# Long convolution and a gated network on one core: the projections of the last 24 tiles as pairs of products with 64 output columns each

## The chip, the cores and the metric

The kernel runs on one core of a Trainium2 chip. A core has five engines that run side by side, each through a list of instructions of its own and in its order: TensorE (matrix products, PE in the profile, with its weight loads listed as PEld), VectorE (DVE), ScalarE (ACT), GpSimd (POOL) and SyncE (SP, which here only issues DMAs). They wait for one another through semaphores. TensorE reads its two operands from SBUF and writes its product to PSUM, which has eight banks of 512 float32 columns on 128 partitions. The metric is the device time of one execution, in microseconds (us); the median over the runs counts.

## The reference

Two blocks are computed one after the other, all in float32. The first is a long convolution; the second is a network of two layers, and the change is in the second.

```python
# first block: x, v are (4, 12480, 128)
h_filt = (np.maximum(pos_emb @ w1, 0.0) @ w2) * np.exp(-0.01 * pos)[:, None]
u = x * v
y = irfft(rfft(u, n=2*S) * rfft(h_filt, n=2*S))[:, :S, :]   # along the sequence
z = (x * y).reshape(49920, 128)
# second block: w_in is (128, 2048), w_out is (2048, 128)
h = z @ w_in
out = (h * np.cos(h)) @ w_out
```

Each of the 49,920 rows of z is multiplied by `w_in` (up to 2048 numbers), goes through h cos h, and is multiplied by `w_out` (down to 128 numbers).

## The kernel before

The convolutions are done as Fourier transforms written as matrix products, one batch entry after the other; their results go to a buffer `zd` in HBM. The network takes these rows in 98 tiles (`NALL` = 98): a tile is up to 128 rows of `zd` with four tokens each, so 512 tokens (416 in tile 0, 352 in tile 97). Inside a tile the 2048 hidden numbers are handled in 16 chunks (`NFC`) of 128.

For one tile, `moe_load` brings the rows into `zb`; `moe_turn` turns them with four transposes on TensorE (features then lie on partitions, tokens along the free dimension) and ScalarE copies them to `at`. For each chunk c:

- `moe_up` (line 740): TensorE multiplies chunk c of `w_in` (the stationary operand, 128x128) by `at` (the moving operand, 128x512) into a bank `ph`. ScalarE scales it and adds a quarter turn (`a`, line 746), VectorE rounds it (`k`, line 749), GpSimd subtracts (`f`, line 752).
- `moe_act` (line 755): ScalarE takes the sine (`cs`, line 757), VectorE multiplies it with `ph` (`gt`, line 759). With this `ph` is free again.
- `moe_down` (line 762): TensorE multiplies chunk c of `w_out` by `gt` and adds to the tile's accumulator, a bank named `acc` or `cv`; chunk 0 starts the sum and chunk 15 ends it.

At the end of a tile `moe_evict` copies the accumulator to `ot`, `moe_back` turns it back with four transposes and `moe_store` sends it out.

The order is written out by hand in one loop over all (tile, chunk) steps (lines 949 to 974). Step i issues the up product of chunk i, then the down product of the chunk four steps earlier (`LAG` = 4), then the sine and the gate of chunk i-1. After chunk 3 come the transposes of the next tile, after chunk 8 those that turn the previous tile's result back. Between the steps the loop issues pieces of the convolutions as long as there are any; by the time of the last 24 tiles they are done, and TensorE has only up products, down products and transposes left. Four banks rotate under the name `ph` (they serve the up products and both kinds of transposes), and four buffers under `gt`. So an up product waits until VectorE has taken the gate of the bank's previous user, and a gate is written only when the down product that read the buffer's previous content is done.

A float32 product is compiled into two passes: weight load, pass, weight load, pass. In the profile one product is therefore two MATMUL and two LDWEIGHTS records; a transpose is one of each. `128*128` in a PE row means 128 rows of the array (contraction) by 128 columns (output partitions), and `128x512` the moving operand.

Of the kernel before, what the change touches and what calls it, by code (L numbers as in the profile page):

```python
# [16 lines left out]
P = 128  # L17
# [13 lines left out]
def kernel(  # L31
# [46 lines left out]
    nc = tc.nc  # L78
# [16 lines left out]
    CB = D // 2  # L95
# [3 lines left out]
    NFC = DFF // P  # L99
# [4 lines left out]
    NALL = 1 + math.ceil((NROWS - R) / P)  # L104
# [608 lines left out]
        yield from i1_units(bank)  # L713


    ats, accs = {}, {}

    def first_row(n):
        return min(R + (n - 1) * P, NROWS) if n else 0
# [1 line left out]
    def rows_of(n):  # L721
        return first_row(n + 1) - first_row(n)
# [17 lines left out]
    def moe_up(pool, n, c):  # L740
        m = G * rows_of(n)
        ph = ps_h.tile([P, BANK], F32, name="ph")
        nc.tensor.matmul(ph[:, 0:m], w_in_sb[:, c * P:(c + 1) * P], ats[n][:, 0:m],  # L743
                         start=True, stop=True)
        a = pool.tile([P, BANK], F32, name="a", bufs=3)
        nc.scalar.activation(a[:, 0:m], ph[:, 0:m], AF.Identity,  # L746
                             bias=quarter[:, 0:1], scale=INV_TWO_PI)
        k = pool.tile([P, BANK], F32, name="k")
        nc.vector.tensor_scalar(out=k[:, 0:m], in0=a[:, 0:m], scalar1=ROUND,  # L749
                                scalar2=ROUND, op0=ALU.add, op1=ALU.subtract)  # L750
        f = pool.tile([P, BANK], F32, name="f")
        nc.gpsimd.tensor_tensor(f[:, 0:m], a[:, 0:m], k[:, 0:m], op=ALU.subtract)  # L752
        return ph, f, m
# [8 lines left out]
    def moe_down(n, c, gt):  # L762
        if c == 0:

            accs[n] = bank() if made[0] == B * NG and n % 2 else \
                ps_acc.tile([P, BANK], F32, name="acc")
        m = G * rows_of(n)
        nc.tensor.matmul(accs[n][:, 0:m], w_out_sb[:, c, :], gt[:, 0:m],  # L768
                         start=(c == 0), stop=(c == NFC - 1))

    def moe_evict(pool, n):
        m = G * rows_of(n)
# [27 lines left out]
    with tc.manual_schedule():  # L800
        with tc.tile_pool(name="psum", bufs=8, space=PSUM) as psum, \
                ExitStack() as first:
            def bank():
                return psum.tile([P, BANK], F32, name="ps")
# [97 lines left out]
            w_in_sb = wpool.tile([D, DFF], F32, name="w_in_sb")  # L902
            w_out_sb = wpool.tile([P, NFC, D], F32, name="w_out_sb")
# [45 lines left out]
        for i in range(len(steps) + LAG):  # L949
            if i < len(steps):  # L950
                n, c = steps[i]
                if n == 0 and c == NFC // 2:
                    load(1)
                if c == NFC - 4 and n + 2 < NALL:
                    load(n + 2)
                hidden[i] = moe_up(mpool, n, c)
            if i >= LAG:
                pn, pc = steps[i - LAG]
                moe_down(pn, pc, gates.pop(i - LAG))
                if pc == NFC - 1:  # L960
                    ots[pn] = moe_evict(mpool, pn)
            if 0 <= i - 1 < len(steps):
                gates[i - 1] = moe_act(mpool, *hidden.pop(i - 1))
            if i < len(steps):

                if c == (LAG - 1 if n else NFC - 2) and n + 1 < NALL:
                    moe_turn(mpool, n + 1)
                if c == NFC // 2 and n - 1 in ots:
                    obs[n - 1] = moe_back(mpool, n - 1, ots.pop(n - 1))
                if c == NFC // 2 + 2 and n - 1 in obs:  # L970
                    moe_store(n - 1, obs.pop(n - 1))
            owed += 1.0
            while owed > 0.0:
                owed -= next(conv, owed)
# [30 lines left out]
```

## Time and profile before

| what | us |
|---|---|
| median of 3 runs (lowest, highest) | 3761.64 (3761.51, 3764.51) |
| span of the profiled execution, first to last instruction | 3758.9 |
| PE busy in it | 3690.6 (98%) |
| PE weight loads busy | 2110.4 (56%) |
| DVE, ACT, POOL busy | 2773.7, 2508.2, 2557.6 |
| mean of one up-product pass, 512 columns moving | 0.593 |
| mean of one POOL subtraction `f` | 1.267 |

For the profiled execution the span is the only time given; it lies 2.7 us under the median of the runs. Busy times are sums of the records of an engine. The records of TensorE overlap, since a pass starts while the one before it is still draining, so what a pass costs is read from the distance between two starts and not from the record's length.

### The profile page before, as it was taken

How to read it: one execution, taken by the hardware profiler on the slowest of the kernel's cores; microseconds unless marked ns; L12 is line 12 of the kernel's file. 1: busy time of each engine (PE TensorE's matmuls, PEld its weight loads, DVE VectorE, ACT ScalarE, POOL GpSimd, SP SyncE). 2: the span in 40 equal slices, each digit the busy share in tenths (PEclk: the TensorE clock that was granted, in tenths of full speed). 3: DMA queues.
4: the chain of work that ended last, by engine and by line, in shares of the span. 5: the costliest groups of instructions: out<-in, count | busy, mean ns of one | idle time of the engine just before them, and what ended most of it. 6: DMA issues, size and time to landing. Idle time of an engine off the chain costs nothing.

```text
span 3758.9 us, 47177 instructions
## 1 busy us (share of the span) xinstructions
PE 3690.6 (98%) x13546; PEld 2110.4 (56%) x13546; DVE 2773.7 (74%) x5586; ACT 2508.2 (67%) x4660; POOL 2557.6 (68%) x2318
## 2 busy tenths in 40 slices
PE   7898999999999999999999999999999999999999
PEld 6777555555566556555565556555566544444444
DVE  8887997687866787788766776788765666666666
ACT  5757776766665557766665567666664677777777
POOL 6666776588845665688745664788644677777776
PEclk9999999999999999999999999999999999999999
DMA  6263551022203650122104530122105200000000
GB/s 167 64 185 107 155 167 33 25 72 79 72 12 91 181 151 12 40 79 77 52 18 128 180 105 21 52 79 76 38 21 172 76 23 17 17 23 18 17 23 13
DMA packets 209499, 276.14 MB, mean 73 GB/s; under 512 B 17111, under 2 KB 146535, under 8 KB 209111
## 3 DMA queue, kind: packets, MB, share of 16 engines
q1 hardware_dynamic: 209239, 273.12, 24.8%
q8 instruction: 109, 1.79, 0.2%
q14 instruction: 151, 1.24, 0.1%
HBM read 193.64 MB, written 79.42 MB: 73 GB/s over the span
## 4 chain that ended last, share of the span: by engine, by line
PE 88%; DVE 3%; POOL 3%; ACT 2%; DMA 2%; issue 1%; SPq 0%; POOLq 0%; DVEq 0%; ACTq 0%
PE ph L743 33%; PE acc L768 28%; PE cv L504 5%; PE cv L768 5%; PE cv L479 4%; PE cv L407 3%; PE cv L448 3%; PE ph L126 2%; POOL f L752 1%; PE ps L407 1%; PE ps L448 1%; DMA tm<-td 1%; DMA wd<-w 1%; ACT cs L757 1%; DVE k L749 1%
## 5 line engine op out<-in xcount | busy, mean ns | idle before, releaser
L752 POOL TENSOR_TENSOR f<-a,k 128x512 f32<-128x512 f32 (+1 forms) x1568 | 1986.2, 1267 | 1060.5 <-DVE k L749 1059.1
L743 PE MATMUL ph<-at,w_in_sb 128*128 128x512 f32 (+1 forms) x3136 | 1599.0, 591 | 3.7 <-DVE gt L759 2.7
L746 ACT ACTIVATE a<-ph,quarter 128x512 f32<-128x512 f32 (+1 forms) x1568 | 1071.2, 683 | 704.8 <-PE ph L743 695.2
L768 PE MATMUL acc<-gt,w_out_sb 128*128 128x512 f32 (+1 forms) x2688 | 1370.3, 591 | 0.0
L759 DVE TENSOR_TENSOR gt<-ph,cs 128x512 f32<-128x512 f32 (+1 forms) x1568 | 1077.3, 687 | 359.9 <-ACT cs L757 341.8
L757 ACT ACTIVATE cs<-f 128x512 f32<-128x512 f32 (+1 forms) x1568 | 981.0, 626 | 366.6 <-POOL f L752 364.3
L749 DVE TENSOR_SCALAR k<-a 128x512 f32<-128x512 f32 (+1 forms) x1568 | 792.9, 506 | 550.7 <-ACT a L746 524.2
L768 PEld LDWEIGHTS acc<-gt,w_out_sb 128*128 128x128 f32 x2688 | 508.4, 189 | 642.8 <-issue 631.9
L743 PEld LDWEIGHTS ph<-at,w_in_sb 128*128 128x128 f32 x3136 | 553.2, 190 | 337.7 <-issue 257.5
L474 POOL TENSOR_TENSOR slots<-slots,t 120x256 f32<-120x256 f32 x384 | 312.9, 821 | 59.9 <-DVE t L467 25.6
L504 PEld LDWEIGHTS cv<-slots,tm 96*104 96x104 f32 x1920 | 238.6, 169 | 106.8 <-issue 85.4
L504 PE MATMUL cv<-slots,tm 96*104 96x128 f32 x1920 | 251.7, 273 | 9.9 <-POOL tm L297 5.0
L768 PE MATMUL cv<-gt,w_out_sb 128*128 128x512 f32 (+1 forms) x448 | 224.5, 583 | 1.0 <-DVE gt L759 1.0
L479 PEld LDWEIGHTS cv<-cs,slots 120*96 120x96 f32 x1536 | 176.7, 167 | 67.2 <-issue 65.2
L479 PE MATMUL cv<-cs,slots 120*96 120x120 f32 x1536 | 183.2, 266 | 0.0
L448 PEld LDWEIGHTS cv<-slots,w 124*120 124x120 f32 x576 | 103.7, 184 | 124.3 <-issue 112.3
L407 PEld LDWEIGHTS cv<-c,slots 104*124 104x124 f32 x768 | 132.6, 192 | 72.2 <-issue 60.0
L448 PE MATMUL cv<-slots,w 124*120 124x256 f32 x576 | 173.0, 380 | 0.0
L407 PE MATMUL cv<-c,slots 104*124 104x192 f32 x768 | 151.8, 327 | 5.4 <-DVE gt L759 3.5
L768 PEld LDWEIGHTS cv<-gt,w_out_sb 128*128 128x128 f32 x448 | 84.9, 190 | 104.8 <-issue 99.5
L489 DVE TENSOR_TENSOR slots<-cv,other 96x240 f32<-96x240 f32 x384 | 133.1, 394 | 1.5 <-ACT other L487 1.4
L395 DVE TENSOR_TENSOR xt<-xt,vt 104x256 f32<-104x256 f32 x177 | 132.6, 751 | 0.6 <-DMA vt<-in_v_dram 0.6
(131 smaller groups left out, 2520.9 us busy)
## 6 DMA issues: line engine op xcount, KB each, us to landing
h<-hd SPq DMA_DIRECT2D x144, 240.0 KB
tm<-td SPq DMA_DIRECT2D x96, 312.0 KB
xt<-in_x_dram SPq DMA_DIRECT2D x120, 208.0 KB
vt<-in_v_dram SPq DMA_DIRECT2D x120, 208.0 KB
xs<-in_x_dram SPq DMA_DIRECT2D x120, 208.0 KB
zd<-zs SPq DMA_DIRECT2D x119, 208.0 KB
zb<-zd SPq DMA_DIRECT2D x96, 256.0 KB
w<-wd SPq DMA_DIRECT2D x144, 116.2 KB
```

The lines of the kernel that those rows point to most:

```text
L407: nc.tensor.matmul(ps[0:KE, i * 2 * N1:(i + 1) * 2 * N1], u[:, b, 0:KE, i], c1[0:u.shape[0], :, :].rearrange("p r k -> p (r k)"), start=Tr ...
L448: nc.tensor.matmul(pi, w[:, i, :], parts[0:KE, :, k], start=True, stop=True)
L474: nc.gpsimd.tensor_tensor(y[:, r], y[:, r], t[:, r], op=op)
L479: nc.tensor.matmul(ps[0:N1, (i * 2 + r) * N2:(i * 2 + r + 1) * N2], parts[0:N2, r, :, b, i], cs[:, r, :], start=True, stop=True)
L504: nc.tensor.matmul(ps[0:R, i * D:(i + 1) * D], t[:, i, r, :], slots[0:N1, :, place, :], start=(r == 0), stop=(r == 1))
L743: nc.tensor.matmul(ph[:, 0:m], w_in_sb[:, c * P:(c + 1) * P], ats[n][:, 0:m], start=True, stop=True)
L746: nc.scalar.activation(a[:, 0:m], ph[:, 0:m], AF.Identity, bias=quarter[:, 0:1], scale=INV_TWO_PI)
L749: nc.vector.tensor_scalar(out=k[:, 0:m], in0=a[:, 0:m], scalar1=ROUND, scalar2=ROUND, op0=ALU.add, op1=ALU.subtract)
L752: nc.gpsimd.tensor_tensor(f[:, 0:m], a[:, 0:m], k[:, 0:m], op=ALU.subtract)
L757: nc.scalar.activation(cs[:, 0:m], f[:, 0:m], AF.Sin, scale=TWO_PI)
L759: nc.vector.tensor_tensor(gt[:, 0:m], ph[:, 0:m], cs[:, 0:m], op=ALU.mult)
L768: nc.tensor.matmul(accs[n][:, 0:m], w_out_sb[:, c, :], gt[:, 0:m], start=(c == 0), stop=(c == NFC - 1))
```

## The change

Three places in the tile count are marked: `PAIRS` = 74, `HALVES` = 82, `TURNED` = 90. Up to tile 73 nothing is changed. From there on some products are split into two halves of 64 output columns: half 0 takes the left 64 columns of the weights and writes PSUM partitions 0 to 63, half 1 takes the right 64 and writes partitions 64 to 127. Both halves stream the same moving operand in full.

- Tiles 74 to 81: up products stay whole. The down product of an even chunk is put off until that of the next, odd chunk; then four halves are issued: (c-1, half 0), (c-1, half 1), (c, half 0), (c, half 1).
- Tiles 82 to 89: up and down products are both split, each chunk at its own step as before.
- Tiles 90 to 97: up products are split as in 82 to 89; down products are put off by pairs of chunks as in 74 to 81, in the order (c-1, half 0), (c, half 1), (c, half 0), (c-1, half 1).

The four transposes of a group stay whole (128 columns) everywhere. In the built program the halves are placed in a TensorE array divided into two parts of 128 rows by 64 columns, at column 0 and at column 64. Each half is again weight load, pass, weight load, pass. The other engines' instructions and their order are the same as before, and so is the number of semaphore waits on each engine.

```diff
+    PAIRS, HALVES, TURNED = NALL - 24, NALL - 16, NALL - 8
 ...
     def moe_up(pool, n, c):
-        nc.tensor.matmul(ph[:, 0:m], w_in_sb[:, c * P:(c + 1) * P], ats[n][:, 0:m],
-                         start=True, stop=True)
+        if n < HALVES:
+            nc.tensor.matmul(ph[:, 0:m], w_in_sb[:, c * P:(c + 1) * P], ats[n][:, 0:m],
+                             start=True, stop=True)
+        else:
+            for h in range(2):
+                nc.tensor.matmul(ph[h * CB:(h + 1) * CB, 0:m],
+                                 w_in_sb[:, c * P + h * CB:c * P + (h + 1) * CB],
+                                 ats[n][:, 0:m], start=True, stop=True)
 ...
     def moe_down(n, c, gt):
-        nc.tensor.matmul(accs[n][:, 0:m], w_out_sb[:, c, :], gt[:, 0:m],
-                         start=(c == 0), stop=(c == NFC - 1))
+        def part(cc, h, gt, start=False, stop=False):
+            nc.tensor.matmul(accs[n][h * CB:(h + 1) * CB, 0:m],
+                             w_out_sb[:, cc, h * CB:(h + 1) * CB], gt[:, 0:m],
+                             start=start, stop=stop)
+
+        if n < PAIRS:
+            nc.tensor.matmul(accs[n][:, 0:m], w_out_sb[:, c, :], gt[:, 0:m],
+                             start=(c == 0), stop=(c == NFC - 1))
+        elif HALVES <= n < TURNED:
+            for h in range(2):
+                part(c, h, gt, c == 0, c == NFC - 1)
+        elif c % 2 == 0:
+            pending[n] = gt
+        else:
+            last = pending.pop(n)
+            four = ((c - 1, 0, last), (c - 1, 1, last), (c, 0, gt), (c, 1, gt)) \
+                if n < TURNED else \
+                ((c - 1, 0, last), (c, 1, gt), (c, 0, gt), (c - 1, 1, last))
+            for i, (cc, h, g) in enumerate(four):
+                part(cc, h, g, c == 1 and i < 2, c == NFC - 1 and i >= 2)
```

More of the change, by code (lines that the diff above doesn't have):

```diff
@@ L713, in forward_units @@
         yield from i1_units(bank)
-    ats, accs = {}, {}
+    ats, accs, pending = {}, {}, {}
+    PAIRS, HALVES, TURNED = NALL - 24, NALL - 16, NALL - 8
     def first_row(n):
```

## The prediction

> **What bounds the kernel now.** I read the page's busy table and slices first, then three windows of eight tiles each (the 24 that change), then TensorE's timeline in them, and last the places where a weight load was not made ahead.
>
> ```profile
> PE 3690.6 (98%) x13546; PEld 2110.4 (56%) x13546; DVE 2773.7 (74%) x5586; ACT 2508.2 (67%) x4660; POOL 2557.6 (68%) x2318
> ...
> PEclk9999999999999999999999999999999999999999
> ```
>
> ```profile
> 3076.80:3303.60 226.80, 226.80 (x578) 103.53 (x577) 146.19 (x256) 176.84 (x281) 162.84 (x129) 1.00 0.07 19
> 3303.60:3530.30 226.70, 226.70 (x577) 103.48 (x576) 145.99 (x256) 176.79 (x281) 162.65 (x129) 1.00 0.07 19
> 3530.30:3758.90 228.60, 222.88 (x585) 104.43 (x583) 144.59 (x259) 173.09 (x284) 159.28 (x130) 1.00 0.06 17
> ```
>
> In the windows (stretch; length, then busy us of PE, weight loads, DVE, ACT, POOL; granted clock, DMA share, GB/s) PE is never idle while the tiles stream, at the full clock. ACT, next, is busy 78% (176.84 of 226.80). A tile costs 226.8/8 = 28.35 us. Whatever TensorE needs more here is added to the end; what the others do is covered up to 22%.
>
> ```profile
> 3600.34 1.02 PE L768 MATMUL acc<-gt,w_out_sb 128*128 128x512 f32 x2
> 3601.20 1.02 PE L743 MATMUL ph<-at,w_in_sb 128*128 128x512 f32 x2
> 3602.05 1.02 PE L768 MATMUL acc<-gt,w_out_sb 128*128 128x512 f32 x2
> 3602.91 0.60 PE L126 MATMUL ph<-ident,ot 128*128 128x128 f32 x4
> 3603.35 1.02 PE L743 MATMUL ph<-at,w_in_sb 128*128 128x512 f32 x2
> ```
>
> Starts are 0.859 us apart per product (two passes of 0.429) and 0.43 per four transposes; 32 x 0.859 + 2 x 0.43 = 28.35. A pass's record is 0.592 long, so 0.163 of it drains under the next pass. Between transposes and products nothing is lost.
>
> ```profile
> 3629.97 0.19 PEld L768 LDWEIGHTS cv<-gt,w_out_sb 128*128 128x128 f32 x1 [0.24 <-issue]
> 3630.40 0.19 PEld L768 LDWEIGHTS cv<-gt,w_out_sb 128*128 128x128 f32 x1 [0.24 <-issue]
> ```
>
> Each load starts with a pass and is done 0.19 later, ahead of its own pass. Where a load could not be made ahead it shows in the product:
>
> ```profile
> 3741.11 0.86 PE L743 MATMUL ph<-at,w_in_sb 128*128 128x352 f32 x2
> 3741.81 0.76 PE L768 MATMUL cv<-gt,w_out_sb 128*128 128x352 f32 x2
> ```
>
> The first waited for a gate with its load: 0.86 against 0.76, so an exposed load of 128 columns costs 0.10. Last, what a pass's length depends on:
>
> ```profile
> L448 PE MATMUL ps<-slots,w 124*120 124x256 f32 x192 | 62.2, 405 | 7.0 <-DVE w L293 6.5
> ...
> L451 PE MATMUL ps<-ftile,w 124*120 124x256 f32 x96 | 29.4, 387 | 0.0
> L357 PE MATMUL ps<-w_sb,slots 128*96 128x256 f32 x120 | 26.1, 379 | 0.8 <-ACT slots L350 0.8
> ```
>
> With 256 elements moving, 96 output columns take 379 ns and 120 take 387 to 405: the moving elements set it, the columns do not. So a half of 64 columns should last as long as a whole product, and all hangs on whether two halves stream beside each other.
>
> **The change, part by part.**
>
> 1. Passes. Split are 8 x 16 = 128 down products in tiles 74 to 81 and 8 x 32 in each of the next two groups: 640 products become 1280 halves, 2560 passes of 0.429 in place of 1280. If the two halves of the array work at once, passes h0-1, h0-2, h1-1, h1-2 (half, pass) come in this order: h0-2 needs h0-1 done, h1-1 can start with h0-2, h1-2 runs beside the next product's h0-1. Two passes always run together and a product still costs 0.859: 0 us. If they run one after the other, 608 x 0.859 + 32 x 0.592 (the 352-column tile, two passes of 0.296) = 541 us. No matmul of before is narrow enough to stand beside another, so the ends are 0 and 541. I take 0: the halves have disjoint columns, disjoint PSUM partitions, no semaphore between them, and the nearest thing in the trace, weight load beside pass, overlaps perfectly.
>
> 2. Half-empty ends. In that pattern the first pass of a run of halves and the last stand alone: n products take 2n + 1 slots. Counting the built order, there are 93 runs between whole products or transposes: 61 of four halves (tiles 74 to 81), 32 longer ones cut by transposes, two groups per tile. 93 x 0.429 = 40 us.
>
> 3. Switching between whole and halved array, 186 times. From below: 0, as between transposes and products. From above: a drained pass and an exposed load, 0.163 + 0.10 = 0.27, so 50 us. I take the 0.163, since a whole product and a half overlap in columns as no two neighbours of before differ: 30 us. The Trainium skill (TensorEngine Tiling (Array Packing), Key Properties) says that changing the tiling mode drains the engine, which no row here can show; it speaks against this change, and by its drain alone the sum would be the same, without it 30 us less.
>
> 4. Weight loads. 1280 loads become 2560 of 64 columns. Two per slot of 0.429 fit even at the 0.19 measured for 128 columns. I take 0. The upper bound is that a load is never made past a pass still waiting: then h1's loads start only when h0-2 has, and each half pays one exposed load, 1280 x 0.05 to 0.10 (half of the 0.10, by columns, or all) = 64 to 128 us.
>
> 5. Waits on gates and banks. By pairs, two ups now stand back to back, then 1.72 us of downs. An up's gate is done 5.02 us after the up starts (timeline: up at 3672.06, a 3673.12, k 3673.91, f 3674.42, cs 3675.72, gt 3676.38 + 0.69 = 3677.07). The tightest taker of a bank comes three ups later with transposes between: before 3 x 1.717 + 0.43 = 5.58. After: two ups 1.72, four halves 1.72 + 0.43 + 0.33 (steps 2 and 3), transposes 0.43, one up 0.86: 5.48, against 5.02 + 0.10 for its load. No stall. Were steps 2 and 3 free it would be 4.72, short by 0.40, three times a tile in 16 tiles: 19 us, the bound; behind the waiting up stand TensorE's downs. GpSimd, 1.27 per chunk, delays the second chunk of a pair by 1.27 - 0.86 = 0.41; its bank is wanted a block of downs later (6.4). The put-off down holds its `gt` until up + 1.72 + 0.43 + 0.16; VectorE wants to overwrite it 4.32 after the previous up's start, 0.3 later: 0. Behind that gate on DVE would stand the next chunk's rounding, and GpSimd behind that.
>
> 6. Tail. The last four halves all follow the last gate: 5 slots of 0.296 in place of 2, 0.9 us. DMAs, stores and the queues of SP and POOL keep their order: 0.
>
> Sum: 0 + 40 + 30 + 0 + 0 + 1 = +71, span 3758.9 to 3830. The median lies 2.7 above the span: 3833 us, 1.9% slower. Own range, with steps 2 to 5 at their ends: 3762 + 40 to 3762 + 110, 3802 to 3872.
>
> The Trainium skill (TensorE: Matmul & The Clock Gate, Measured speedup vs the span model) gives 2.38x for three column tiles of 512 elements, 0.79 of the ideal. An estimate with that efficiency on all 640 products, 640 x 0.859 x (1/0.79 - 1), would be +146 us. No run here shows it, and step 1 is not taken from it.
>
> **The rivals.**
>
> - Loads in strict order (step 4's bound): +71 + 64 to 128, 3897 to 3961. For it: in this trace no load ever starts before the pass ahead of it has. Against it: there was never a second place to load into, so that row can't tell.
> - Half overlap: h1-1 runs beside h0-2, but h1-2 doesn't stand beside the next product's first pass. Three slots per product: 608 x 0.429 + 32 x 0.296 = 270, plus the 30 of switching: 4062. For it: ups wait on semaphores at their first load. Against: whole products with the same waits follow each other without a gap.
> - No overlap: +541, plus 0 to 30: 4303 to 4333. Gates would then all be early and TensorE still the bound. For it: every two passes in the trace are a full 0.429 apart. Against: all of them need the same columns.
> - Not slower: passes of 64 columns are shorter than 0.429. It decides from the point where 640 x 0.859 = 550 us shrinks by 71, a pass of 0.374. Against it the equal times at 96 and 120 columns; I know of nothing for it. At a pass of 0.35 the time would be 3833 - 550 x 0.185 = 3731.
>
> **How the numbers follow.** Overlap with costs at the ends 0.48, strict loads 0.22, half overlap 0.10, no overlap 0.15, not slower 0.05. The time is the first one's, 3833. The range leaves out no overlap and not slower, 0.20, and runs from the first one's lower end less a few us for a clock or start that differs to half overlap's: 3795 to 4065. A measurement of this kernel tells about 0.2% (7.5 us) from no change; every case but the last is slower by more, and the last I split: faster 0.03, same 0.02, slower 0.95.
>
> **What would show it.** The same three windows, by tiles: if I am right the first eight take 226.8 + 61 x 0.755 = 273 us, the next two 8-tile groups 16 x 0.755 = 12 more each (0.755 = 0.429 + 2 x 0.163), with starts of half 1's first pass and half 0's second within some 0.01. Strict loads: those starts 0.05 to 0.10 apart, 0.05 to 0.10 per half on top, 13 to 26 in the first group and 26 to 51 in each of the others. Half overlap: 1.29 per split product; no overlap: 1.72, and the second group 447 us or more. Step 3 shows in the first start after each run, step 5 as idle PE before an up, released by `gt`. I am wrong if half passes are not 0.429, if which `gt` the two halves read matters (then the third group differs from the second), or if the granted clock falls with both halves busy.

## The result, and the profile after

The changed kernel takes 3799.45 us (median; 3796.12 to 3800.12) against 3763.07 for the kernel before (3761.51 to 3765.24): 1.0097 times as long, 95% interval 1.0083 to 1.0111, so 31 to 42 us more. The forecast was slower, 3833 us in a range of 3795 to 4065. The direction and the mechanism (halves run beside each other) hold; the predicted rise of 71 us is about twice the 36 measured.

The page of the profile after, engine totals and TensorE's granted clock:

```profile
PE 3725.2 (98%) x14826; PEld 2036.1 (54%) x14826; DVE 2808.1 (74%) x5586; ACT 2493.7 (66%) x4660; POOL 2561.5 (68%) x2318
...
PEclk9999999999999999999999999999999999999999
```

1280 more passes than before (14826 against 13546), and yet only 34.6 us more of PE busy time; the clock is unchanged. The next view is TensorE's timeline of the changed kernel, cut to the transposes that turn the next tile: the first number is the start in us, and the distance of two such lines is one tile. The pairs stand in tiles 74 to 81, 82 to 89 and 90 to 97.

```profile
3111.73 0.66 PE L126 MATMUL ph<-ident,zb 128*128 128x128 f32 x4
3143.43 0.66 PE L126 MATMUL ph<-ident,zb 128*128 128x128 f32 x4
...
3361.84 0.65 PE L126 MATMUL ph<-ident,zb 128*128 128x128 f32 x4
3390.78 0.65 PE L126 MATMUL ph<-ident,zb 128*128 128x128 f32 x4
...
3593.80 0.66 PE L126 MATMUL ph<-ident,zb 128*128 128x128 f32 x4
3623.19 0.66 PE L126 MATMUL ph<-ident,zb 128*128 128x128 f32 x4
```

31.70, 28.94 and 29.39 us a tile, where before it is 28.34:

```profile
3112.03 0.60 PE L126 MATMUL ph<-ident,zb 128*128 128x128 f32 x4
3140.37 0.60 PE L126 MATMUL ph<-ident,zb 128*128 128x128 f32 x4
```

Most of the loss is in the first group, where whole and halved products alternate; in the second group all products are halved and a tile loses 0.60.

Where a tile of the first group loses it, in the same timeline, with the weight loads (PEld) below:

```profile
3175.13 0.66 PE L126 MATMUL ph<-ident,zb 128*128 128x128 f32 x4
3175.62 1.02 PE L745 MATMUL ph<-at,w_in_sb 128*128 128x512 f32 x2
3176.89 1.12 PE L745 MATMUL ph<-at,w_in_sb 128*128 128x512 f32 x2 [0.24 <-ACT at L738]
...
3177.94 1.94 PE L777 MATMUL cv<-gt,w_out_sb 128*64 128x512 f32 x8
3179.81 1.98 PE L745 MATMUL ph<-at,w_in_sb 128*128 128x512 f32 x4
```

```profile
3177.94 0.20 PEld L777 LDWEIGHTS cv<-gt,w_out_sb 128*64 128x64 f32 x4 [0.76 <-issue]
3178.42 0.14 PEld L777 LDWEIGHTS cv<-gt,w_out_sb 128*64 128x64 f32 x2 [0.29 <-issue]
3178.85 0.14 PEld L777 LDWEIGHTS cv<-gt,w_out_sb 128*64 128x64 f32 x2 [0.28 <-issue]
3179.81 0.30 PEld L745 LDWEIGHTS ph<-at,w_in_sb 128*128 128x128 f32 x2 [0.81 <-DVE k L756]
```

Three things are to be seen. First, eight half-passes (`x8`) take 1.94 us from first start to last end, where four whole passes take 1.88 in a row (four starts 0.429 apart and 0.592 for the last): two halves cost one whole product. Four loads start within 0.06 us at 3177.94, then two per 0.43. The passes themselves start 0.006 to 0.007 us apart in pairs (3177.942 and 3177.949, 3178.422 and 3178.429, 3178.852 and 3178.858, 3179.281 and 3179.287). Eight passes fill four slots, not the five that the prediction counted: there is no half-empty slot at either end. Second, around the run of halves time goes to the switch: from the last whole pass at 3177.42 to the first half it is 0.52 in place of 0.429, the first half slot is 0.48, the last one to the next load 0.53, and the first whole pass after it 0.53 because its load is exposed. The four excesses are 0.093, 0.051, 0.098 and 0.104: about 0.345 us per run. Around a group of transposes inside halved tiles (the lines below) they are 0.098, 0.055, 0.093 and 0.051: 0.297. Third, the second up product behind the transposes starts at 3176.89 and not at 3176.48; it waits for ScalarE's copy `at`, and its exposed load makes it 1.12 long.

```profile
3447.70 1.03 PE L777 MATMUL cv<-gt,w_out_sb 128*64 128x512 f32 x4
3448.66 0.66 PE L126 MATMUL ph<-ident,zb 128*128 128x128 f32 x4
3449.24 1.08 PE L749 MATMUL ph<-at,w_in_sb 128*64 128x512 f32 x4
```

At the end of the kernel three of the last four halves (six passes) follow the last gate (`gt`). First the changed kernel, then the one before:

```profile
3787.80 1.40 PE L777 MATMUL cv<-gt,w_out_sb 128*64 128x352 f32 x6 [0.40 <-DVE gt L766]
3789.74 0.64 PE L126 MATMUL ph<-ident,ot 128*88 128x128 f32 x4 [0.54 <-ACT ot L800]
```

```profile
3752.86 0.86 PE L768 MATMUL cv<-gt,w_out_sb 128*128 128x352 f32 x2 [0.35 <-DVE gt L759]
3754.27 0.64 PE L126 MATMUL ph<-ident,ot 128*88 128x128 f32 x4 [0.54 <-ACT ot L774]
```

From the first pass behind that gate to the last transposes it takes 1.94 us in place of 1.41, 0.5 more.

| in the changed kernel | count | us each | us |
|---|---|---|---|
| switches around a run of four halves (tiles 74 to 81) | 61 | 0.345 | 21.0 |
| switches around transposes (from tile 82 on) | 32 | 0.297 | 9.5 |
| waits of up products behind transposes, per tile, tiles 74 to 81 | 8 | 0.60 | 4.8 |
| the same, tiles 90 to 96 (behind tile 97 no tile is left to turn) | 7 | 0.45 | 3.2 |
| the end, behind the last gate | 1 | 0.5 | 0.5 |
| sum | | | 39.0 |

(0.60 is 31.70 - 28.34 - 8 x 0.345; 0.45 is 29.39 - 28.94.) From the transposes in tile 73 to the end the two profiled executions differ by 39.1 us; up to there, where nothing is changed, the one after was 3.7 us shorter.

### The profile page after: what moved, and what is told of

Its sections match the earlier page's. It is cut to its first block, busy times and chain, and to the rows that moved or that the text cites. A ratio compares the mean times of both kernels' runs of the same rounds, so it can differ in the third digit from the quotient of the medians.

```text
span 3794.3 us, 49737 instructions
## 1 busy us (share of the span) xinstructions
PE 3725.2 (98%) x14826; PEld 2036.1 (54%) x14826; DVE 2808.1 (74%) x5586; ACT 2493.7 (66%) x4660; POOL 2561.5 (68%) x2318
## 4 chain that ended last, share of the span: by engine, by line
PE 88%; DMA 3%; DVE 3%; POOL 2%; ACT 2%; issue 1%; SPq 0%; POOLq 0%; DVEq 0%; ACTq 0%
PE ph L745 29%; PE acc L782 24%; PE ph L749 5%; PE cv L504 5%; PE acc L777 4%; PE cv L479 4%; PE cv L777 4%; PE cv L448 3%; PE cv L407 3%; PE ph L126 2%; DMA hd<-h 2%; POOL f L759 1%; PE ps L407 1%; PE ps L479 1%; PE cv L782 1%
## 5 line engine op out<-in xcount | busy, mean ns | idle before, releaser
L745 PE MATMUL ph<-at,w_in_sb 128*128 128x512 f32 (+1 forms) x2624 | 1341.2, 595 | 5.5 <-ACT at L738 2.7
L756 DVE TENSOR_SCALAR k<-a 128x512 f32<-128x512 f32 (+1 forms) x1568 | 836.5, 533 | 559.9 <-ACT a L753 529.9
L782 PE MATMUL acc<-gt,w_out_sb 128*128 128x512 f32 (+1 forms) x2304 | 1174.1, 591 | 0.0
L782 PEld LDWEIGHTS acc<-gt,w_out_sb 128*128 128x128 f32 x2304 | 435.4, 189 | 552.2 <-issue 542.1
L745 PEld LDWEIGHTS ph<-at,w_in_sb 128*128 128x128 f32 x2624 | 453.2, 189 | 255.5 <-issue 137.3
L749 PE MATMUL ph<-at,w_in_sb 128*64 128x512 f32 (+1 forms) x1024 | 252.5, 588 | 1.7 <-DVE gt L766 0.6
L777 PE MATMUL acc<-gt,w_out_sb 128*64 128x512 f32 x768 | 188.1, 596 | 0.0
L777 PE MATMUL cv<-gt,w_out_sb 128*64 128x512 f32 (+1 forms) x768 | 185.0, 585 | 0.6 <-DVE gt L766 0.6
L749 PEld LDWEIGHTS ph<-at,w_in_sb 128*64 128x64 f32 x1024 | 70.1, 137 | 134.9 <-issue 101.8
```

Of the source, the lines that this page charges most:

```text
L749: nc.tensor.matmul(ph[h * CB:(h + 1) * CB, 0:m], w_in_sb[:, c * P + h * CB:c * P + (h + 1) * CB], ats[n][:, 0:m], start=True, stop=True)
L777: nc.tensor.matmul(accs[n][h * CB:(h + 1) * CB, 0:m], w_out_sb[:, cc, h * CB:(h + 1) * CB], gt[:, 0:m], start=start, stop=stop)
```

## The experiments

Three questions were open: is the rest really switches and nothing that halves cost by themselves; what is the wait behind the transposes; and why are the ends of a run not half empty, that is, in what order does TensorE take the passes. The theory was that each part of the divided array goes through its own instructions; the rivals are in the expectations. Where nothing else is said the edit is against the changed kernel, and a tile's time is the distance between its transposes as above.

### The transposes' bank

```diff
 def moe_turn(pool, n):
-        pt = ps_h.tile([P, BANK], F32, name="ph")
+        pt = bank() if n > PAIRS else ps_h.tile([P, BANK], F32, name="ph")
```

> Theory (switches and one bank): of the 39 us that the profile of the changed kernel has over before, about 8 are a wait of the second up product behind a tile's transposes, which takes over the transposes' bank and waits until ScalarE has copied it. Taking that bank from the three that are free by then removes the wait: tiles 74 to 81 go from 31.69 us to 31.1 to 31.2 (8 runs of halves at 0.345 on 28.34), tiles 90 to 97 from 29.39 to 28.94, tiles 82 to 89 stay at 28.94; the median falls by 7 to 8 us, to about 3792. Rival (the wait is for gates that come late because down products stand in pairs, or for the longer block of halves): the bank makes no difference, 3799 and the same tile times.

Measured: 3792.83 us, 1.0082 times before (1.0067 to 1.0097), 6.6 under the changed kernel. Its timeline, one tile of the first and one of the third group:

```profile
3111.76 0.66 PE L126 MATMUL cv<-ident,zb 128*128 128x128 f32 x4
3142.94 0.66 PE L126 MATMUL cv<-ident,zb 128*128 128x128 f32 x4
...
3618.98 0.66 PE L126 MATMUL cv<-ident,zb 128*128 128x128 f32 x4
3648.04 0.65 PE L126 MATMUL cv<-ident,zb 128*128 128x128 f32 x4
```

The first pair reads 31.18, the second 29.06; the second group of tiles stays at 28.94. So the theory holds: 0.5 us a tile in the first group and 0.33 in the third were the wait for that bank. What is left, 0.08 and 0.12, stands at the up product right behind the other transposes (those of `ot`), which waits for a gate; this is read from the timeline, no run takes it away in halves.

### By pairs, but whole

```diff
-    PAIRS, HALVES, TURNED = NALL - 24, NALL - 16, NALL - 8
+    PAIRS, HALVES, TURNED = NALL - 24, NALL, NALL
 ...
-        if n < HALVES:
+        if True:
 ...
-            for i, (cc, h, g) in enumerate(four):
-                part(cc, h, g, c == 1 and i < 2, c == NFC - 1 and i >= 2)
+            for cc, g in ((c - 1, last), (c, gt)):
+                nc.tensor.matmul(accs[n][:, 0:m], w_out_sb[:, cc, :], g[:, 0:m],
+                                 start=(cc == 0), stop=(cc == NFC - 1))
```

> Whole products everywhere, only the order by pairs is kept, in all of the last 24 tiles. Theory: no switch is left, and only the wait for the transposes' bank remains, 0.5 to 0.6 us a tile: tiles at 28.9, 3763 + 12 to 15 = 3775 to 3778. Rival 1 (the halves' blocks make the wait): tiles at 28.34 and 3763. Rival 2 (step 5 of the prediction, gates late three times a tile by 0.40): tiles at 29.5, 3792.

Measured: 3787.75 us, 1.0069 (1.0054 to 1.0084), 29.44 us a tile in all three groups: 1.10 a tile, neither the 0.6 of the theory nor the 1.2 of rival 2. The timeline shows two waits, not one:

```profile
3351.86 0.60 PE L126 MATMUL ph<-ident,zb 128*128 128x128 f32 x4
3352.30 1.02 PE L745 MATMUL ph<-at,w_in_sb 128*128 128x512 f32 x2
3353.71 1.12 PE L745 MATMUL ph<-at,w_in_sb 128*128 128x512 f32 x2 [0.38 <-ACT at L738]
3354.67 1.88 PE L795 MATMUL cv<-gt,w_out_sb 128*128 128x512 f32 x4
...
3360.68 0.60 PE L126 MATMUL ph<-ident,ot 128*128 128x128 f32 x4
3361.46 1.13 PE L745 MATMUL ph<-at,w_in_sb 128*128 128x512 f32 x2 [0.18 <-DVE gt L766]
```

The second up behind the first transposes starts 1.41 us after the one ahead of it in place of 0.86, and its load is exposed (1.12 against 1.02): 0.65. The first up behind the other transposes starts 0.78 after them in place of 0.43, with its load exposed: 0.45. The sum is the 1.10. In the changed kernel only 0.60 of the 1.10 is left. That its switches cover the rest, because they give the late copies and gates time, is argued and was not tested by itself. So by pairs costs more without halves (25 us over 24 tiles) than the waits cost with them.

Whether that is all was tried with the same kernel and both kinds of transposes in free banks (the same line is changed in `moe_turn` and in `moe_back`; the edit is against the run just above):

```diff
-        pt = ps_h.tile([P, BANK], F32, name="ph")
+        pt = bank() if n > PAIRS else ps_h.tile([P, BANK], F32, name="ph")
```

> The run with whole products and down products by pairs, but both kinds of transposes take a bank of the three that are free by then, so that the four banks of the up products rotate among up products alone. Theory (by pairs costs nothing but the two waits for banks behind the transposes, 0.65 and 0.45 us a tile, which are gone): tiles at 28.34 in place of 29.44, the median back at 3762 to 3764, no change from before. Rival (two up products in a row bring the gates late wherever they stand): part of the 1.10 us a tile stays, with waits for gates at other up products; tiles between 28.6 and 29.4, 3769 to 3788.

Measured: 3762.62 us, 1.0000 (0.9990 to 1.0009).

```profile
3368.94 0.60 PE L126 MATMUL cv<-ident,zb 128*128 128x128 f32 x4
3397.28 0.60 PE L126 MATMUL cv<-ident,zb 128*128 128x128 f32 x4
```

28.34 a tile, as before, from the third of the 24 tiles on. The first two take 28.81 and 28.82: there the transposes of `ot` still take one of the up products' banks (the `n > PAIRS` of the edit), and the 0.47 is their wait again. The order by pairs is free once the up products' banks are not lent to transposes; all its cost was banks.

### All halves, and how the cost goes with runs

In all 24 tiles up and down are split at each chunk (`PAIRS, HALVES, TURNED = NALL - 24, NALL - 24, NALL`):

> Up and down products split at each chunk in all of the last 24 tiles. Theory (each half of the array goes through its own instructions, so a run of halves has no half-empty end, and costs only its two switches, 0.297 us between transposes): 28.94 us in all 24 tiles, 24 x 0.60 = 14 us, 3777. Rival (half-empty ends of 0.429 per run, as predicted, hidden in the changed kernel by something): 24 x 2 x (0.297 + 0.429) = 35 us, 3798. Rival (two halves cost more than one whole product by a few ns each): the excess would be 768 products times that, on top of 14.

Measured: 3775.93 us, 1.0036 (1.0022 to 1.0050). The windows view of one tile (stretch; length, busy us of PE, loads, DVE, ACT, POOL; clock, DMA share, GB/s):

```profile
3371.02:3399.96 28.94, 28.94 (x138) 9.85 (x136) 18.03 (x33) 22.31 (x36) 20.48 (x17) 1.00 0.06 19
```

28.94 a tile (28.89 the first), two switched runs at 0.297 a tile and no more: 32 products a tile in halves cost nothing by themselves. Then the same with the up products whole (and `if True:` in `moe_up`), so that each tile has 16 runs of two halves:

> Up products whole, down products split at each chunk, in the last 24 tiles: 16 runs a tile of two halves in place of 8 runs of four. Theory (a run costs its two switches, 0.345 us, however long it is): tiles at 28.34 + 16 x 0.345 = 33.86, 3763 + 132 = 3895. Rival (the cost goes with the number of halves, 0.345/4 for each): 28.34 + 32 x 0.086 = 31.1, 3829. Rival (half-empty ends): 28.34 + 16 x (0.429 + 0.163 to 0.33) = 37.8 to 40.5, 3990 to 4055.

Measured: 3894.07 us in one run, 33.83 us a tile.

```profile
3439.57 1.12 PE L745 MATMUL ph<-at,w_in_sb 128*128 128x512 f32 x2
3440.62 1.08 PE L777 MATMUL acc<-gt,w_out_sb 128*64 128x512 f32 x4
3441.63 1.12 PE L745 MATMUL ph<-at,w_in_sb 128*128 128x512 f32 x2
3442.69 1.08 PE L777 MATMUL acc<-gt,w_out_sb 128*64 128x512 f32 x4
```

A chunk takes 2.06 in place of 1.717, 0.345 for its run of two, the same as for a run of four. The cost goes by runs, not by halves. Here no two ups stand together, and no wait is left.

The counter-test keeps the array halved through a whole tile: the transposes too are done as products of 64 columns with the identity. The edit is against the run with all halves; the turns of tiles up to 74 and of the last one keep `transpose`, and `moe_back` calls the same `turn_block`.

```diff
+    def turn_block(n, dst, src):
 ...
+            for h in range(2):
+                nc.tensor.matmul(dst[h * CB:(h + 1) * CB], src[:, h * CB:(h + 1) * CB],
+                                 ident[0:k, 0:k], start=True, stop=True)
 ...
-            transpose(pt[:, i * m:(i + 1) * m], zb[0:m, i, :], ident)
+            turn_block(n, pt[:, i * m:(i + 1) * m], zb[0:m, i, :])
```

> Up and down in halves in the last 24 tiles, and the transposes too, as products of 64 columns with the identity (two passes of 128 elements for each, two halves beside each other; those of the first turn and of the last tile stay as they were). Then the array stays halved from tile to tile. Theory (the 0.60 us a tile are the four switches and nothing else): they go, and each group of transposes takes 4 x 2 x 0.1085 = 0.868 in place of 0.434: 28.34 + 2 x 0.434 = 29.21 us a tile, 3763 + 24 x 0.87 = 3784. Rival (halves cost 0.60 a tile by themselves): 28.94 + 0.87 = 29.81, 3798. Rival (the extra cost stands at any change between products of one kind and another): the same 29.81.

Measured: 3786.74 us in one run.

```profile
3403.58:3432.79 29.21, 29.21 (x162) 10.94 (x160) 17.84 (x32) 22.39 (x36) 20.21 (x16) 1.00 0.07 19
```

29.21 a tile, the theory's figure: the 0.60 is the switches and nothing else. It is gone, and the two groups of transposes, dearer by 0.43 each, add 0.87 to the 28.34.

### What runs beside what

The left half of each up product is done twice in tiles 82 to 89 (extra work; nothing is left out):

```diff
-    PAIRS, HALVES, TURNED = NALL - 24, NALL - 16, NALL - 8
+    PAIRS, HALVES, TURNED = NALL - 16, NALL - 16, NALL
 ...
-            for h in range(2):
+            for h in (0, 0, 1) if n < NALL - 8 else (0, 1):
```

> Up and down in halves in tiles 82 to 97; in tiles 82 to 89 the up product's left half is done twice, so its halves come as left, left, right. Theory (what runs beside each other are different columns): the left columns need two products in a row, each up costs 1.717 in place of 0.859: tiles 82 to 89 at 28.94 + 16 x 0.859 = 42.7 us, 110 us in all; tiles 90 to 97 at 28.94; 3763 + 5 + 110 + 5 = 3883. Rival (neighbouring passes run in pairs whatever their columns, so that the two passes of one half stand beside each other): six passes take three slots, 28.94 + 16 x 0.429 = 35.8, 3828. Rival (twice the left columns is hidden): 28.94, 3773.

Measured: 3879.08 us in one run, 42.66 a tile with the left half twice.

```profile
3398.98 0.66 PE L126 MATMUL ph<-ident,zb 128*128 128x128 f32 x4
3441.64 0.65 PE L126 MATMUL ph<-ident,zb 128*128 128x128 f32 x4
```

Passes on the same columns follow one another at 0.429; what stands beside is the other half. This also says which passes the pairs 0.007 apart are: the two first passes of half 0 and half 1, although half 0's second pass stands between them in the program. Then with quarters of 32 columns in tiles 82 to 89 (the edit is against the kernel before; tiles 74 to 81 are in halves, 90 to 97 whole):

```diff
+    def cuts(n):
+        return 2 if PAIRS <= n < HALVES else 4 if HALVES <= n < TURNED else 1
 ...
+        q = P // cuts(n)
+        for h in range(cuts(n)):
+            nc.tensor.matmul(ph[h * q:(h + 1) * q, 0:m],
+                             w_in_sb[:, c * P + h * q:c * P + (h + 1) * q], ...
```

(the down products alike)

> Up and down in halves of 64 columns in tiles 74 to 81, in quarters of 32 columns in tiles 82 to 89, whole in tiles 90 to 97. Theory (columns that do not overlap run beside each other, as many as there are): quarters cost what halves cost, 28.9 us a tile, a little less for the shorter exposed load of 32 columns (0.027 in place of 0.05 at two switches a tile); 3763 + 5 + 5 = 3773. Rival (two at a time is all): a product of quarters takes 1.717, 28.94 + 32 x 0.859 = 56.4 us a tile, 3993. Rival (passing the four times two instructions costs a few ns each): up to some 10 ns x 32 products, 0.3 us a tile.

Measured: 3772.95 us in one run; 28.91 us a tile with quarters, 28.94 with halves, 28.34 whole.

```profile
3384.50 1.06 PE L749 MATMUL ph<-at,w_in_sb 128*32 128x512 f32 x8
3385.38 1.04 PE L778 MATMUL acc<-gt,w_out_sb 128*32 128x512 f32 x8
3386.24 1.04 PE L749 MATMUL ph<-at,w_in_sb 128*32 128x512 f32 x8
```

Eight passes of 512 in 0.86 us: four at a time.

### How far ahead TensorE reaches

Two kernels with whole ups and downs by pairs in halves; the moving operand in one, two or four pieces in the three groups. In the first the halves stand in turn, in the second all of half 0 comes ahead of all of half 1 (of the two `for` lines each kernel has one; the product inside the loop is left out here):

```diff
+            size = BANK if n < HALVES else BANK // 2 if n < TURNED else BANK // 4
+            both = ((c - 1, pending.pop(n)), (c, gt))
+            pieces = [(a, min(a + size, m)) for a in range(0, m, size)]
+            for cc, g, a, z, h in [(cc, g, a, z, h) for cc, g in both
+                                   for a, z in pieces for h in range(2)]:      # in turn
+            for cc, g, a, z, h in [(cc, g, a, z, h) for h in range(2)
+                                   for cc, g in both for a, z in pieces]:      # half 0 first
```

> Up products whole, down products by pairs of chunks in halves in all of the last 24 tiles, half 0 and half 1 in turn; the moving operand in one piece of 512 in tiles 74 to 81, in two of 256 in tiles 82 to 89, in four of 128 in tiles 90 to 97. It is the measure for the next run. Theory: a half-pass lasts as long as its moving elements take, and its weight load is hidden: 31.7 us a tile in all three groups, as in tiles 74 to 81 of the changed kernel. With 128 elements a pass is 0.108 us and two loads at 0.05 fill it, so a few us a tile may come on top in the third group.

> The same products as in the run beside it, but all of half 0 of a pair of chunks ahead of all of half 1: half 1's first pass then has 4, 8 and 16 passes (with their loads 8, 16 and 32 instructions) of half 0 ahead of it in the three groups. Theory (each half of the array goes through its own instructions, whatever stands ahead of them for the other half): the same times as with the halves in turn, 31.7 us a tile. Rival (a pass can be taken ahead of a few waiting ones only): the group in which the reach ends and those after it grow, by up to 8 x 1.72 = 13.7 us a tile, to 45. Rival (strict order, a pass never passes a waiting one): 8 x (1.72 - 0.43) = 10.3 us more in the first group, to 42, and 12 to 14 more in the others.

Measured, one run each: in turn 3843.38 us, tiles at 31.69, 31.76 and 31.91; half 0 first 3977.32 us, tiles at 31.78, 38.97 and 42.70. The theory without a limit falls with the second group, strict order with the first. The timeline of the run with half 0 first, one run of halves of the second and one of the third group; the windows are cut so that a line ends with the pass named below:

```profile
3464.66 1.08 PE L786 MATMUL cv<-gt,w_out_sb 128*64 128x256 f32 x4
...
3464.66 2.86 PE L786 MATMUL cv<-gt,w_out_sb 128*64 128x256 f32 x16
...
3703.16 1.52 PE L786 MATMUL cv<-gt,w_out_sb 128*64 128x128 f32 x12
...
3703.16 3.33 PE L786 MATMUL cv<-gt,w_out_sb 128*64 128x128 f32 x32
```

In the second group four passes of half 0 run alone (`x4`, 0.216 apart), and with the fifth, 0.006 us after it, half 1's first starts: of 8 + 8 passes, half 1's first is the ninth in the program, four behind the fifth. In the third group twelve run alone, and half 1's first, the 17th, starts with the 13th: four behind again. In the first group it is the fifth and starts 0.013 us after the first. So TensorE takes a pass ahead of up to three waiting ones for other columns, and no further. What counts is the passes that wait, not the place in the program: in the run with quarters the fourth quarter's first pass is the seventh of its product and starts 0.02 us after the first, ahead of the second passes of three quarters. The price fits: 12 slots in place of 8 make 4 x 0.216 x 8 runs = 6.9 of the 7.2 measured, and 28 in place of 16 make 12 x 0.109 x 8 = 10.5 of 10.8.

No kernel of these is faster than the kernel before by more than its runs differ.

## Why the prediction was right or wrong, point by point

- What bounds: right. In tiles 82 to 89 TensorE is never idle, as before; in tiles 74 to 81 it is busy 31.3 to 31.5 of 31.70 us, the rest being the wait behind the transposes. Each excess on it came through to the end.
- Step 1, passes at no cost: right. Halves beside each other cost 0.859 per product as a whole one does (the run with all halves and the one with halved transposes leave nothing over). Of the three signs of being wrong none came: half passes are 0.429 apart, the clock stays at 1.00, and which `gt` the halves read does not matter, since the third group's excess over the second is nearly all one bank (29.06 against 28.94 without it).
- Step 2, half-empty ends, 40 us: this is the step that failed. It measured 0. The working took the passes in the order of the program, with half 1's first pass behind half 0's second. TensorE takes it ahead: its first starts 0.007 after half 0's first. The run with half 0 first shows the lone slots that step 2 had in mind, but only where more than three passes wait ahead. The 40 us were also the one cost that was given no lower end.
- Step 3, switches, 30 us at 0.163: measured 30.5, as 186 half switches of 0.15 to 0.17, so the size was right, but by luck, for what it is made of was not: each is 0.09 to 0.10 in which nothing starts, and a first load that is exposed, 0.05 for a half or a transpose and 0.10 for a whole product. The estimate had taken the draining tail of 0.163 alone. That changing the tiling mode drains the engine, as the Trainium skill says (TensorEngine Tiling (Array Packing), Key Properties), agrees with the 0.09 to 0.10 here, and with the run with halved transposes, where the array stays divided from tile to tile and the cost is absent. That the engine is emptied is not shown: the load behind a run starts 0.065 us ahead of the end given for the run's last pass (3179.808 against 3179.281 + 0.592), and such ends are modelled.
- Step 4, loads at no cost: right for 512 elements moving. With 128 elements (third group of the pieces in turn) a slot is still 0.109, two loads of 64 columns in each.
- Step 5, waits at 0, bound 19 us: mis-sized; it measured 8 (4.8 + 3.2). It also looked at the wrong taker: it supposed that the banks go round strictly, and that the third up behind needs the gate. The bank of the transposes goes to the second up behind them, which waits for ScalarE's copy `at`; the waits in the profile of before had the trace of it, there without a loss (us in total, times, longest):

```profile
PEld ph L743 <- ACT at L737: 8.1, 23, 0.4
```

  And the gate wait that it had in mind is real: without switches it is 0.45 a tile, once, not three times 0.40.
- Step 6, the tail: 0.9 forecast, 0.5 measured. Only three of the last four halves run behind the last gate, and they take four slots in place of two, not five.
- The rivals: strict loads, half overlap and no overlap are all excluded by 28.94 us a tile in the second group (447 us for the group was the price of no overlap; it took 232). Not slower is excluded by the interval.
- The sum: 71 forecast, 36 measured in the medians, 39 in the profile; 40 too much from step 2, 8 too little from step 5. That the time lies in the range is partly luck. The forecast's own case ran from 3802 to 3872, and 3799.45 lies below it; only the few us taken off for clock and start, down to 3795, let it in. The wait that step 5 put at nothing did the rest: with most of it taken away the run with the transposes' bank took 3792.83, under the range.

## What to carry to other kernels

Two float32 products of 64 output columns on the two halves of the array, or four of 32, run at the price of one, with the same or with different moving operands; splitting a product that already fills 128 columns gains nothing, and every change between the whole and the divided array costs here 0.15 to 0.17 us. So narrow products are best put beside each other in long runs, with the halves in turn in the program (a pass with no more than three waiting ones ahead of it). An estimate from these figures, not run here: a lone pair of narrow products that would otherwise take 0.859 each saves 0.859 and pays 0.345 for its two switches. And where an order on a saturated engine is changed, look up which buffer each instruction takes over: here the whole cost of a reordering, 25 us, was two banks lent to transposes.

## What was not expected

- TensorE starts a pass ahead of others that stand before it in the program, if its part of the array is free: 0.47 us ahead of half 0's second pass in the changed kernel. The Trainium skill (TensorE: Matmul & The Clock Gate, The mechanism) has matmuls start in the order of the program; the measurement decides. The reach is three waiting passes with their loads: with half 0 first, at a distance of 4 passes the halves start 0.013 us apart, at 8 and 16 half 1 starts only when the distance has shrunk to 4.
- Four quarters run beside each other as well as two halves do: 28.91 us a tile against 28.94.
- The costs of the parts do not add: the order by pairs alone costs 25 us in 24 tiles, 1.10 a tile, but 0.60 a tile together with halves.
